# Five waits and positions in a kernel of attention and two expert layers: where output rows, gathered blocks, router transposes, weight turns and one router step stand

## The chip, the cores and the metric

The kernel runs on 1 core of a Trainium2 chip. The metric is device time in microseconds (us), the median of several runs. TensorE, VectorE, ScalarE and GpSimd are the core's compute engines (PE, DVE, ACT and POOL in the profile; PEld is TensorE's weight load); SyncE (SP) only issues transfers here.

## What is computed

The reference, cut to its core (4 batches, 8 heads, 512 local and 32 global positions, head size 64; 2,176 tokens of 512 values in all; 2,048 inner values in the first layer, 8 experts of 1,024 in the second):

```python
a = attention(q_l, k_l, v_l, q_g, k_g, v_g)   # window of 32, plus global keys
x = a.transpose(0, 2, 1, 3).reshape(2176, 512)
h = x @ w_in
x = (np.maximum(h, 0) + alpha * np.minimum(h, 0)) @ w_out
logits = x @ w_gate                            # 8 experts
for idx in np.argsort(-logits.flatten()):      # greedy, 272 tokens an expert
    tok, e = idx // 8, idx % 8
    if assigned[tok] < 0 and counts[e] < 272:
        assigned[tok] = e; counts[e] += 1
for e in range(8):
    out[assigned == e] = np.maximum(x[assigned == e] @ w1[e], 0) @ w2[e]
```

## The kernel before, in words

Every product of the two layers is made in three matmuls: an operand is split into a rounded high half and a low half (the helper `split`, lines 72 and 73: a cast on ScalarE, then a subtract on GpSimd or VectorE), and high times high, low times high and high times low are added up in PSUM. The 2,176 tokens are worked in 8 chunks of 272.

The stages, in the order of time. First attention, then mixed with the first half (`hf` 0) of the first layer. When attention is done (about 223 us) the remaining chunks of half 0 go on, and beside them the weights of half 1 are decoded from 64-bit numbers (`decoding`, lines 77 to 93: a load, one ScalarE and four VectorE instructions into a tile `mag`, which has two buffers) and split. They come in 16 parts: 8 of `w_in`, then 8 of `w_out`. The loop at lines 659 to 676 takes one part after every fifth yield of the GEMM generator (a yield comes after six matmuls). A `w_out` part also returns two closures: `turn_` (line 132: four transposes of the decoded part into `wt`, TensorE, and a ScalarE copy) and `mul_` (line 139: its product with the gate weights, `wp`). They go into the list `more` and are run from its front when it is longer than a limit; what is left runs after the loop. The order of TensorE in this stage, and that of all other engines in every later stage, is made by a scheduler at build time from planned durations, with program order as priority.

Next the first GEMM of half 1 for all 8 chunks (`gemm1b`), with logits of the router (`logits` line 284; `lput`, lines 287 to 297: ScalarE copies to `Lrow`, transposes on TensorE into `l`, a VectorE reduction). Then its second GEMM (`gemm2b`, L1195), in two passes of two output tiles, each over eight operand tiles `f`. From here on the order of TensorE is that of the program. The list `post` holds closures (the last chunk's `lput`, then each chunk's row transposes) that are run behind certain operand tiles.

Mixed into it is the router: eight phases, each picking one expert and its tokens by a threshold search of six steps (`pc`, L907, and `pa`, L919), then `pq` and, but for the last, `pr` (L986), which carries the count of tokens taken; the list of an expert's tokens (`pl` L852, `ps` L859) follows within the next phase. It is a generator that yields planned times in us: `WB` and `WA` around the search steps, `WQ` before `pq`, `WR0` (first phase) or `WR` before `pr`, `WL` in the listing. The GEMM generators yield 0.113 a matmul, and `advance` takes that off the router's planned time; at zero its next instructions are emitted.

Last come eight expert slots. Slot `k` has 8 tiles `up` (L1068, 12 matmuls each) and 4 tiles `down` (L1084, 24 each). Behind the first up tiles it emits the output rows of slot `k - 1` (`emit`): two blocks of four transposes (`ox`, L1115; one PSUM buffer for both), a ScalarE copy into `orow` (L1116) and a scatter on GpSimd's queue (L1118). At the beginning of a slot the token rows of the next are fetched (`fetch_x`, L1018, GpSimd's queue, one buffer `xg`); they are turned in three blocks by `gather` (`xt`, L1054), which begins when the slot's planned time `n` is over `GA` and at least 5 after the fetch, with 2.2 between blocks. Each block is split to `xsh` (ScalarE) and `xsl` (VectorE). The weights of later slots are loaded and split meanwhile (`fetch_1`, `fetch_2`: casts on ScalarE, subtracts on GpSimd). Before slot 0 TensorE runs matmuls of no use (`idle`, L108) while the first rows arrive.

Of the kernel before, what the change touches and what calls it, by code (L numbers as in the profile page):

```python
# [25 lines left out]
def tile_attention_moe_moe(ctx: ExitStack, tc: tile.TileContext, qkw, vw,  # L26
# [133 lines left out]
    def loadx(c, hf):  # L160
        cs = slice(c * CH, (c + 1) * CH)
        X[c, hf] = [None, None]
        if hf:
            t = gx.tile([128, 2, KD, CH], F32, name="xb", bufs=2)
            for i, src in enumerate((xs, xpart)):
                nc.sync.dma_start(out=t[:, i], in_=src[:, :, cs].rearrange("k p t -> p k t"))
                X[c, hf][i] = t[:, i]
# [10 lines left out]
    post = []  # L178
# [21 lines left out]
    def gemm(c, hf, nxt):  # L200
        if len(X[c, hf]) < 3:
            splitx(c, hf)
        if nxt is not None:
            loadx(*nxt)
        gh = gt_.tile([128, KH, CH], F32R, name="ghi", tag="ghi")
        gl = gt_.tile([128, KH, CH], F32R, name="glo", tag="glo")
        wo = WO[hf]
        for f in range(KH):
            g = gh_.tile([128, CH], F32, name="g")
            yield from gemm1(c, hf, f, g)  # L210
            split(gh[:, f], gl[:, f], g, lo_eng=P)
            if post:
                post.pop(0)()
            yield 0.7
        if (c + 1, hf) in X:
            splitx(c + 1, hf)
        ys = {}
        for d, fs in [(0, range(KH - 2)), (1, range(KH - 2)), (0, range(KH - 2, KH)), (1, range(KH - 2, KH))] + [
                (d, range(KH)) for d in range(2, KD)]:
            if d not in ys:  # L220
                ys[d] = ybank[0].tile([128, CH], F32, name="y", tag=ybank[1])
            ps = ys[d]
            ds_ = slice(d * 128, (d + 1) * 128)
            for f in fs:
                for i, (w, x) in enumerate(((0, gh), (0, gl), (1, gh))):
                    T.matmul(ps, wo[:, w, f, ds_], x[:, f], start=f == 0 and i == 0, stop=f == KH - 1 and i == 2)  # L226
                if f % 2 == 1 and f < KH - 1:
                    yield 0.7
            if fs[-1] < KH - 1:
                continue  # L230
            xd = gx.tile([128, CH], F32, name="xd", bufs=2)
            A.copy(xd, ps)
            nc.sync.dma_start(out=xpart[d, :, c * CH:(c + 1) * CH], in_=xd)
            yield 0.7
        X[c, hf] = None
# [78 lines left out]
    with ExitStack() as at:  # L314
# [308 lines left out]
        c = 0  # L623
        g = None
        going = True
        while going:
# [12 lines left out]
            else:  # L639
# [4 lines left out]
                else:  # L644
                    spent["g"] += x
                    if parts:
                        f, i = parts.pop(0)
# [7 lines left out]
    with tc.tile_pool(name="dc2", bufs=1, side="right") as dc, tc.tile_pool(name="pW", bufs=2, space=PSUM) as pW, \  # L655
            tc.tile_pool(name="pO", bufs=2, space=PSUM) as pO:
        odd.append((pO, "h3"))
        more = []
        parts = [(win_part, i) for i in range(2 * KD)] + [(wout_part, i) for i in range(KH)]
        n = 0  # L660
        while c < NCH:
            if g is None:
                if (c, 0) not in X:
                    loadx(c, 0)
                g = gemm(c, 0, (c + 1, 0) if c + 1 < NCH else None)
            while next(g, None) is not None:
                n += 1
                if n % 5 == 0 and parts:
                    f, i = parts.pop(0)
                    with tc.issue_after(epi[0].ins):  # L670
                        todo = f(dc, 1, i)
                    while len(more) > 2:
                        more.pop(0)()
                    more += todo or []
            g = None
            c += 1
        for f, i in parts:
            more += f(dc, 1, i) or []
        for f in more:
            f()  # L680
    NDEF = 8
    DEF = list(range(NCH - NDEF, NCH))
    with ExitStack() as mo:
# [144 lines left out]

        listed, closed = [0], [0]
        WB, WA = (1.7, 2.7, 1.8, 1.8, 1.8, 1.8), (1.7, 1.3, 1.3, 1.3, 1.3, 1.3)  # L830
        WQ, WR0, WR, WL = 2.7, 6.0, 4.2, 1.2

        def listing(k, pos):
            ra = rt.tile([128, NT], F32, name="ra")
# [261 lines left out]
        def turned(k, m):  # L1096
            d = SLOT[k]
            for q, (a, b) in enumerate(SEG):
                if m == 0:
                    pool, tag = ((px, "tx"), (pm, "sm"), (pm, "sm"))[q]  # L1100
                    d["t", q] = pool.tile([128, DM], F32, name="ox", tag=tag)
                T.transpose(d["t", q][:, m * 128:(m + 1) * 128], tail["o"][:, m] if q == 2 else d["o"][:, m, a:b], ident)
# [22 lines left out]
        def slot(k):  # L1125
            d = SLOT[k]
            d["h"] = (sl.tile([128, K3, CAP], F32R, name="hh"), sl.tile([128, K3, CAP], F32R, name="hl"))
            em = emit(k - 1) if k else iter(())
            for f in range(K3):
                yield from up(k, f)  # L1130
                yield 0.113
                if f < 4:
                    yield next(em, 0)
            d["up"] = True
            d["o"] = sl.tile([128, KD, CAP], F32, name="ot")
            if k == 0:
                tail["o"] = sl.tile([128, KD, 128], F32, name="otail", bufs=1)
            for m in range(KD):
                for i, x in enumerate(down(k, m)):
                    if k == E - 1 and m and i == 15:  # L1140
                        turned(k, m - 1)
                    yield x
                yield 0.113
            if k == E - 1:
                turned(k, KD - 1)
# [17 lines left out]
        HB = {}  # L1163
        NB0 = 12
        SLK, SLK2 = 1.0, 1.0
        GA = 17.5
        mo.enter_context(tc.manual_schedule(engines={mybir.EngineType.PE}))

        def splitg(c, f):
            h, l = (gr[:, t, (KH * DEF.index(c) + f) % NR] for t in range(2))  # L1170
            split(h, l, gbt(c, f), lo_eng=P)
            HB.setdefault(c, []).append((h, l))
# [6 lines left out]
        def gemm2b(c):  # L1179
            xo = X[c, 1]  # L1180
            nxt = [lambda f=f: splitg(c + 1, f) for f in range(KH)] if c + 1 < NCH else []
            if nxt:
                loadp(c + 1)
            wo = WO[1]
            end = c == NCH - 1
            if "x" not in tail:
                tail["x"] = gb_.tile([128, KD, 16 * (NCH - 1)], F32, name="xtail")
            for d2 in range(0, KD, 2):
                ps = [(p4 if d2 else pH).tile([128, CH], F32, name="h2", tag="h4" if d2 else "h1") for _ in range(2)]

                def step(f, j):
                    hi, lo = HB[c][f]
                    ds_ = slice((d2 + j) * 128, (d2 + j + 1) * 128)
                    for a, (w, x) in enumerate(((0, hi), (0, lo), (1, hi))):
                        T.matmul(ps[j], wo[:, w, f, ds_], x, start=f == 0 and a == 0, stop=f == KH - 1 and a == 2)  # L1195
                        if a < 2 or not j:
                            yield 0.113

                def add(j):
                    V.tensor_tensor(xo[:, d2 + j], ps[j], xo[:, d2 + j], op=OP.add)  # L1200

                if end and d2:
                    for j in range(2):
                        for f in range(KH):
                            for x in step(f, j):
                                yield None if j else x
                            if j and f == 4:
                                last_blocks(xo, range(KD - 1))
                        add(j)
                    last_blocks(xo, [KD - 1])  # L1210
                    last_out()
                    return
                for f in range(KH):
                    for j in range(2):
                        yield from step(f, j)
                    if (f % 2 == 1 if c != DEF[0] else d2 or f) and post:
                        post.pop(0)()
                        yield 0.4
                    if nxt and ((d2 == 0 and f % 2) or (d2 and f >= 2)):
                        nxt.pop(0)()  # L1220
                    yield 0.113
                for j in range(2):
                    add(j)
            for q in range(3):
                post.append(lambda q=q: rows(c, xo, q))
            if c == NCH - 2:
                post.append(tails)
# [53 lines left out]
        for k in range(E):  # L1281
# [3 lines left out]
            for x in slot(k):  # L1285
# [3 lines left out]
                nx = SLOT.get(k + 1, {})  # L1289
                if gath is None and "at" in nx and n > GA and n > nx["at"] + 5.0:  # L1290
                    gath = gather(k + 1)
# [94 lines left out]
```

## Time and profile before

| | us |
|---|---|
| median of 3 runs | 852.39 (851.32 to 853.04) |
| the profiled execution | 849.98 |
| its span, first to last instruction | 848.2 |
| TensorE busy in it | 807.7 |
| VectorE, ScalarE, GpSimd busy | 473.8, 388.7, 348.7 |

The profile is of one execution. A row of the waits says who waited, for whom, how long in all, how many times, and the longest; only waits over 0.15 us are counted. A row of the timeline has the start, the duration, the engine, the line, the operation with its tiles and shapes, how many were merged, and in brackets the idle time before it and what ended it. A matmul's end is modelled, and successive matmuls overlap.

### The profile page before, as it was taken

What the parts mean: (1) busy time and instruction counts of PE and PEld (TensorE: products, weight loads), DVE (VectorE), ACT (ScalarE), POOL (GpSimd) and SP (SyncE); (2) the same over time, 40 slices, a digit from 0 to 9 for tenths busy, and PEclk for the clock granted to TensorE, in tenths of its full rate; (3) what the DMA queues carried; (4) which work ended last, traced back from release to release, by engine and by line L of the source; (5) the groups of instructions that cost most, each with busy time, mean ns of one, the idle gap of its engine ahead of it and who ended that gap; (6) DMA issues with size and microseconds to landing.
All of it is one profiled execution on the core that took longest, in us unless ns stands there. A gap on an engine that the chain in (4) does not pass through costs nothing. (4 is left out here: it accounts for less than half of the span.)

```text
span 848.2 us, 21036 instructions
## 1 busy us (share of the span) xinstructions
PE 807.7 (95%) x8380; PEld 742.6 (88%) x8380; DVE 473.8 (56%) x1672; ACT 388.7 (46%) x970; POOL 348.7 (41%) x299
## 2 busy tenths in 40 slices
PE   6989999999998999999999999999899999899995
PEld 4767788988998999998989899998689999899995
DVE  5899955464299741252433466776577677711120
ACT  5786655574455643322322434341355544454431
POOL 1134322020255632120000638470599868778601
PEclk9999999999999999999999999999999999999998
DMA  9975552531355302013221227242376655656201
GB/s 343 384 283 199 192 163 70 216 128 48 109 151 168 111 28 80 27 54 90 69 58 50 81 66 263 65 139 81 90 220 205 185 180 163 195 152 210 91 26 38
DMA packets 47993, 115.99 MB, mean 137 GB/s; under 512 B 4183, under 2 KB 20951, under 8 KB 45847
## 3 DMA queue, kind: packets, MB, share of 16 engines
q1 hardware_dynamic: 44999, 105.73, 38.5%
q0 software_dynamic: 2896, 8.92, 3.2%
q8 instruction: 66, 1.08, 0.5%
q14 instruction: 32, 0.26, 0.1%
HBM read 96.80 MB, written 17.83 MB: 135 GB/s over the span
## 5 line engine op out<-in xcount | busy, mean ns | idle before, releaser
L192 PE MATMUL h<-xh,win 128*128 128x272 f32 x768 | 162.4, 298 | 3.1 <-ACT win L72 1.2
L73 POOL TENSOR_TENSOR m<-raw,m 128x1024 fp32r<-128x1024 f32 x64 | 151.8, 2397 | 18.0 <-ACT m L72 10.0
L192 PEld LDWEIGHTS h<-xh,win 128*128 128x128 f32 x768 | 125.1, 190 | 12.7 <-issue 5.1
L192 PE MATMUL h<-xl,win 128*128 128x272 f32 x384 | 111.7, 292 | 1.4 <-DVE xl L73 1.4
L73 POOL TENSOR_TENSOR glo<-g,ghi 128x272 fp32r<-128x272 f32 x64 | 54.5, 857 | 139.3 <-ACT ghi L72 137.8
L226 PE MATMUL y<-ghi,wout 128*128 128x272 f32 x512 | 109.5, 298 | 1.4 <-ACT wout L72 1.4
L1195 PE MATMUL h<-gr,wout 128*128 128x272 f32 x768 | 108.6, 294 | 0.0
L1068 PE MATMUL h<-xsh,m 128*128 128x272 f32 x512 | 106.0, 295 | 0.4 <-ACT xsh L72 0.4
L1084 PE MATMUL h<-hh,m 128*128 128x272 f32 x512 | 102.8, 293 | 0.0
L73 POOL TENSOR_TENSOR gr<-gb,gr 128x272 fp32r<-128x272 f32 x64 | 48.1, 775 | 132.1 <-ACT gr L72 131.5
L1195 PEld LDWEIGHTS h<-gr,wout 128*128 128x128 f32 x768 | 99.4, 189 | 0.6 <-ACT gr L72 0.4
L226 PEld LDWEIGHTS y<-ghi,wout 128*128 128x128 f32 x512 | 83.0, 188 | 6.8 <-issue 3.6
L197 ACT ACTIVATE neg<-h 128x272 f32<-128x272 f32 x128 | 49.8, 395 | 80.9 <-PE h L192 79.0
L1068 PEld LDWEIGHTS h<-xsh,m 128*128 128x128 f32 x512 | 82.4, 188 | 1.5 <-issue 0.8
L1084 PEld LDWEIGHTS h<-hh,m 128*128 128x128 f32 x512 | 81.7, 188 | 1.3 <-issue 1.3
L72 ACT CAST m<-raw 128x1024 fp32r<-128x1024 f32 x64 | 65.4, 1048 | 29.2 <-DMA raw<-in_moe_w_dram 29.1
L1084 PE MATMUL h<-hl,m 128*128 128x272 f32 x256 | 75.4, 295 | 0.0
L1068 PE MATMUL h<-xsl,m 128*128 128x272 f32 x256 | 74.4, 291 | 1.0 <-issue 0.6
L192 PEld LDWEIGHTS h<-xl,win 128*128 128x128 f32 x384 | 72.9, 190 | 2.2 <-DVE xl L73 2.2
L226 PE MATMUL y<-glo,wout 128*128 128x272 f32 x256 | 73.8, 291 | 0.9 <-POOL glo L73 0.9
L198 DVE SCALAR_TENSOR_TENSOR gb<-neg,al,h 128x272 f32<-128x272 f32 x64 | 31.5, 496 | 76.3 <-ACT neg L197 64.4
L400 ACT ACTIVATE pr<-sc,mx 128x128 f32<-128x128 f32 x128 | 49.9, 392 | 32.3 <-DVE mx L398 32.3
(233 smaller groups left out, 1522.0 us busy)
## 6 DMA issues: line engine op xcount, KB each, us to landing
raw<-in_moe_w_dram SPq DMA_DIRECT2D x64, 512.0 KB, 3.7
vv<-in_v_dram SPq DMA_DIRECT2D x16, 1024.0 KB, 8.4
qk<-in_qk_dram SPq DMA_DIRECT2D x14, 720.0 KB, 8.3
raw<-in_moe_w_in_dram SPq DMA_DIRECT2D x16, 512.0 KB, 5.6
raw<-in_moe_w_out_dram SPq DMA_DIRECT2D x16, 512.0 KB, 3.8
xs<-xb SPq DMA_DIRECT2D x16, 272.0 KB, 6.3
xpart<-xd SPq DMA_DIRECT2D x32, 136.0 KB, 3.1
xb<-xs SPq DMA_DIRECT2D x8, 544.0 KB, 3.9
```

The source lines that it names most:

```text
L72: a = A.copy(hi, src)
L73: return a, (lo_eng or V).tensor_tensor(lo, src, hi.bitcast(F32), op=OP.subtract)
L192: T.matmul(ps, wi[:, w, k, fs], x[:, k], start=i == 0, stop=i == 3 * KD - 1)
L197: A.activation(out=neg, in_=ps, func=AF.Relu, scale=-1.0)
L198: epi[0] = V.scalar_tensor_tensor(g, neg, al1[:, hf * KH + f:hf * KH + f + 1], ps, op0=OP.mult, op1=OP.add)
L226: T.matmul(ps, wo[:, w, f, ds_], x[:, f], start=f == 0 and i == 0, stop=f == KH - 1 and i == 2)
L400: A.activation(out=d["pr", j][:, ii], in_=sc, func=AF.Exp, bias=d["mx", j][:, ii:ii + 1], scale=-1.0, accum_out=d["sm", j][:, ii:ii + 1])
L1068: T.matmul(ps, d["w1"][:, w, kk, fs], x[:, kk], start=i == 0, stop=i == 3 * KD - 1)
L1084: T.matmul(ps, d["w2"][:, w, f, ms], x[:, f], start=i == 0, stop=i == 3 * K3 - 1)
L1195: T.matmul(ps[j], wo[:, w, f, ds_], x, start=f == 0 and a == 0, stop=f == KH - 1 and a == 2)
```

## The change

Five numbers or conditions change, each at its own place:

```diff
@@ decoding the weights of half 1 @@
-                    while len(more) > 2:
+                    while len(more) > 4:
                         more.pop(0)()
                     more += todo or []
@@ the router's planned times @@
-        WQ, WR0, WR, WL = 2.7, 6.0, 4.2, 1.2
+        WQ, WR0, WR, WL = 2.7, 6.0, 5.7, 1.2
@@ slot @@
                 yield from up(k, f)
                 yield 0.113
-                if f < 4:
+                if f % 2 == 0:
                     yield next(em, 0)
@@
-        GA = 17.5
+        GA = 15.5
@@ gemm2b @@
-                    if (f % 2 == 1 if c != DEF[0] else d2 or f) and post:
+                    if (f % 2 == 1 if c != DEF[0] else d2 or f > 3) and post:
                         post.pop(0)()
                         yield 0.4
```

The limit of the list of turns and products goes from 2 to 4 entries. The planned time before `pr` is 1.5 longer in the phases after the first. The second block of a slot's output rows is emitted behind up tile 3 of the next slot (counted from 1) where it was behind tile 2. The gathering of the next slot's rows may begin at 15.5 where it was 17.5. In the first chunk of the second GEMM the waiting closure (the last chunk's `lput`) runs behind the fifth operand tile where it ran behind the second.

## Rows read from the trace of the kernel before

**Rows 1.** The page's first part: busy us (share of the span) xinstructions.
```profile
PE 807.7 (95%) x8380; PEld 742.6 (88%) x8380; DVE 473.8 (56%) x1672; ACT 388.7 (46%) x970; POOL 348.7 (41%) x299
```

**Rows 2.** Waits of TensorE, 604 to 840 us: total, times, longest.
```profile
PE ox L1115 <- ACT orow L1116: 1.8, 3, 0.8
PE pl L852 <- DVE sbs L847: 1.4, 1, 1.4
PE pr L986 <- DVE r L981: 1.2, 2, 0.7
PE pa L919 <- DVE sat L912: 0.8, 1, 0.8
PE pc L907 <- DVE gs L873: 0.7, 1, 0.7
PE h L1068 <- issue: 0.6, 1, 0.6
```

**Rows 3.** Waits of TensorE, 362 to 604 us.
```profile
PE l L296 <- ACT Lrow L291: 1.7, 1, 1.7
```

**Rows 4.** Waits of TensorE, 220 to 362 us.
```profile
PE h L192 <- DVE xl L73: 1.4, 2, 1.0
PE wt L135 <- DVE mag L92: 1.4, 1, 1.4
```

**Rows 5.** The chain of waits, slots 2 and 5: start, us, what.
```profile
680.63 0.38 PE pc L907 x9
...
771.52 6.43 PE h L1084 x51
```

**Rows 6.** Timeline of TensorE around the start of slot 1.
```profile
633.59 0.29 PE L1084 MATMUL h<-hl,m 128*128 128x272 f32 x1
...
634.81 0.42 PE L1054 MATMUL xt<-ident,xg 16*128 16x16 f32 x4
635.66 0.39 PE L1068 MATMUL h<-xsh,m 128*128 128x272 f32 x1 [0.43 <-ACT xsh L72]
636.44 0.39 PE L1068 MATMUL h<-xsl,m 128*128 128x272 f32 x1 [0.38 <-DVE xsl L73]
```

**Rows 7.** Timeline of ScalarE, 471 to 477 us.
```profile
471.27 4.57 ACT L72 CAST gr<-gb 128x272 fp32r<-128x272 f32 x14
475.74 0.43 ACT L291 COPY Lrow<-lp 128x144 f32<-128x144 f32 x2
```

**Rows 8.** Timeline of GpSimd, 471 to 483 us.
```profile
471.77 10.20 POOL L73 TENSOR_TENSOR gr<-gb,gr 128x272 fp32r<-128x272 f32 x14 [105.39 <-ACT gr L72]
```

**Rows 9.** Line 859, the router's listings: min/median/max ns, first to last start.
```profile
L859 PE MATMUL ps<-lb,spread x8: 182/183/197, 534.6 to 742.7; 128*128 128x48 bf16 x8
```

**Rows 10.** Slot 6: PE, PEld, DVE, ACT, POOL busy, PEclk, DMA.
```profile
784.90:812.45 27.55, 26.73 (x214) 26.34 (x213) 5.05 (x11) 10.75 (x22) 13.95 (x9) 1.00 0.21 66
```

**Rows 11.** Timeline of ScalarE at the start of slot 5.
```profile
759.92 1.05 ACT L72 CAST m<-raw 128x1024 fp32r<-128x1024 f32 x1
...
761.15 0.58 ACT L1116 COPY orow<-ox 128x512 f32<-128x512 f32 x1
```

**Rows 12.** Timeline of TensorE: the first turn and a late product.
```profile
270.39 0.66 PE L135 MATMUL wt<-ident,mag 128*128 128x128 f32 x4 [1.40 <-DVE mag L92]
...
354.64 0.95 PE L142 MATMUL wp<-ag,wts 128*128 128x8 f32 x8
```

**Rows 13.** Timeline of VectorE, 264 to 272 us: decoding.
```profile
265.62 0.69 DVE L90 SCALAR_TENSOR_TENSOR mag<-raw,mag 128x512 int32<-128x512 int32 x1
...
266.96 0.42 DVE L85 TENSOR_SCALAR mag<-mag 128x512 f32<-128x512 f32 x1
...
267.88 1.73 DVE L90 SCALAR_TENSOR_TENSOR mag<-raw,mag 128x512 int32<-128x512 int32 x1
```

**Rows 14.** Timeline of GpSimd: a weight subtract and the next stage's constants.
```profile
267.78 1.28 POOL L73 TENSOR_TENSOR win<-mag,win 128x512 fp32r<-128x512 f32 x1 [2.47 <-ACT win L72]
...
360.56 0.13 POOL L703 IOTA ip<- 128x1 int32 x1 [16.87 <-PE wp L142]
```

## The prediction

> **What bounds the kernel now.** I read the page's busy times first: TensorE is busy 807.7 us of a span of 848.2, and no other engine comes near [rows 1]. So the end is set by TensorE's own stream of matmuls, and the question is only which gaps in that stream go or come. Next I read the waits of TensorE in three stretches. Between 604 and 840 us, the eight expert slots, they are few and small: 1.8 us before the second block of output transposes (ox) waiting for ScalarE's copy of the first; 1.2 before pr; 2.9 before the router's other matmuls (pl 1.4, pa 0.8, pc 0.7); 0.6 filed under "issue" [rows 2]. Between 362 and 604 us there is 1.7 us before the router's last put of logits is transposed (l) [rows 3]. Between 220 and 362 us there is 1.4 us before the first weight turn (wt) and 1.4 before operand halves (xl) [rows 4].
>
> What is a gap worth? In a run of 51 matmuls that took 6.43 us one starts every 0.126 us [rows 5], while a single one is shown 0.29 us long [rows 6]. A matmul after a gap starts only after the one before it has ended as well, so a gap that vanishes returns about 0.29 - 0.126 = 0.16 us on top of its idle time.
>
> **The change, part by part.** TensorE's order is written out by hand from the second GEMM of the later half on, with 0.113 planned us for a matmul. I followed the generators with the old and the new numbers; counts of matmuls below come from that.
>
> *Router's transposes.* The last chunk's put (copies to Lrow, then the l transposes) now stands behind 30 matmuls of the second GEMM, not 12. The wait ends when ScalarE has done 14 casts (from 471.27, 4.57 us) and then the Lrow copies, to 476.17 [rows 7]. The 18 matmuls that move ahead of it take 18 x 0.126 = 2.3 us, more than the 1.7 us waited [rows 3, 5]. They need GpSimd's subtracts of the third to fifth tile: 14 took 10.2 us, 0.73 each [rows 8], against 6 x 0.126 = 0.76 of matmuls a tile, so they come just in time and may cost some tenths. Gain 1.75 + 0.16, less 0.2: **1.7 us**; at worst 0, if ScalarE's copies are ordered later by as much. The router starts 18 matmuls later in the stream.
>
> *Longer wait for pr.* From the second phase on pr stands 1.5/0.113 = 13 matmuls later, 1.7 us by 0.126. The two waits seen are 1.2 together, the longer 0.7 [rows 2], so both fit. Gain 1.2 + 2 x 0.16 = **1.5 us**. What queues behind pr on TensorE is the next phase's pc, at the same distance from it, and VectorE's update of the remaining places. The router as a whole ends later by 6 x 1.7 plus the 2.3 above, 12.5 us. Its eight listings run from 534.6 to 742.7 us, and the last is wanted by the slot that starts at 812.45, 70 us after it [rows 9, 10]; the planner never has to force a step. Lateness itself costs nothing. But about one pc (0.38 us for nine) and one pl [rows 5] leave the stretch where TensorE only passes time on idle matmuls and enter slot 0: **-0.5 us**.
>
> *Output rows.* The second ox block moves from behind tile 1 to behind tile 3, 12 matmuls or 1.5 us. In slot 5 a cast of 1.05 us stood on ScalarE ahead of the copy of 0.58, which ended at 761.73 [rows 11]; the longest of the three waits is 0.8 [rows 2], so 1.5 covers it with 0.7 to spare. The scatter behind it moves too, on GpSimd's queue; it stands there behind weight subtracts in every slot and nothing reads its rows. Gain 1.8 + 3 x 0.16 = **2.3 us**, at worst 0 if ScalarE puts another cast ahead.
>
> *Gathered blocks.* They start 2.0 planned us, 18 matmuls, earlier. Their last block then stands 23 matmuls before a slot's end, not 5, and 14 before the end of slot 0, where it stood at the very end. There the first up matmul waited 0.43 us for the high half and the next 0.38 for the low half: 1.2 us from the transposes' end at 635.23 to the low half's use at 636.44 [rows 6]. 14 matmuls give 1.77 us, 23 give 2.9. The 0.6 under "issue" [rows 2] is the same wait in slot 3, by its place two matmuls into the slot. Gain 0.43 + 0.38 + 0.59 + 3 x 0.16 = **1.9 us**; 0.2 off, since slot 0 has only 0.6 us to spare and router work on VectorE can stand in front. GpSimd's next row fetches wait for these transposes (the gathered tile has one buffer) and so also come 2.3 us sooner; the weights they share the queue with are a slot ahead, so that is worth nothing.
>
> *Weight turns.* The list holds two entries a part, so a limit of 4 instead of 2 turns each part one step later (five yields, 30 matmuls, 3.8 us), not two. The first turn, at 270.39, waited 1.40 us for VectorE's decode [rows 12]; one step later the decode is done. Gain 1.4 + 0.16 = **1.6 us**. But the decoded tile (mag) has two buffers, and a part's decode waits for the turn two parts before it: it too starts a step later, on VectorE, and SP's queue holds the raw loads behind the decodes. Three parts, not two, are left when the steps end, and the last one's decode waits for a turn that stands behind all remaining chunks: the whole chain then runs at about 355 us or later, where a leftover product stands now: 3.4 us of decode (from 266.96 to the turn's start), a turn of 0.66, a product of 0.95 [rows 12, 13]. The constants of the next stage already wait for these products (GpSimd 16.87 us) [rows 14]. I cost this at 0.3, since the up matmuls of the next stage cover it and VectorE is slack there; without that cover it is the chain itself, 3.4 + 0.66 + 0.95 = 5 us.
>
> What remains uncosted is how the router's other waits (2.9 us now) fall once every phase lies elsewhere in its slot. The nearest rows are those waits; from -2.9 (all gone) to +12. I take +0.4: the router now stays until the end of slot 4, one slot longer.
>
> **Sum.** -1.7 - 1.5 + 0.5 - 2.3 - 1.7 - 1.6 + 0.3 + 0.4 = -7.6 us. The profiled execution took 849.98 us (span 848.2), so it would become 842.4; it lies 2.4 below the median of the runs shown, 852.39, against which I state the time: **844.8 us**. A measurement of this kernel tells about 0.2%, 1.7 us, from no change.
>
> **A rule against the trace.** VectorE's third decode instruction took 1.73 us in one part and 0.69 in another [rows 13]; beside the first GpSimd's subtract of the previous part ran from 267.78 to 269.06 [rows 14]. Moving decodes by a step changes which of them meet a subtract: between no collision and one more, 1.0 us a part, for five parts. The Trainium skill (SBUF — State Buffer, section "Who interferes with whom") says that a VectorE instruction with two SBUF inputs and a GpSimd instruction that reads SBUF exclude each other for the whole instruction. By that rule the later decodes would be stretched whenever they meet GpSimd's subtracts of the first GEMM; the row agrees that such a stretch exists. What it would do to the time is the first rival.
>
> **Rivals.**
> 1. *The weight turns give nothing back or cost.* Decodes a step later run into GpSimd's subtracts, 5 x 1.0 us on an engine that is already late there (the xl waits, 1.4 us [rows 4]), or TensorE stands for the last part's chain of 5 us. For it: the list of three left over. Against it: the next stage has slack on all engines but TensorE. The gain of 1.6 goes and some 3 come: 844.8 + 4.6 = 849.4.
> 2. *ScalarE closes the gaps again.* Its order is made by a scheduler from planned durations. If weight casts of 1.05 us [rows 11] again stand ahead of the copies of ox and of the gathered halves, 2.3 + 1.7 go: 848.8.
> 3. *Slower: the router's waits multiply.* In slots 0 to 4 each phase has twelve pc and pa, a pl and a ps, each tied to a fixed count of matmuls after VectorE's work. At the new places they meet the slot's own VectorE work. If each of five phases had one wait of each size now seen (1.4 + 0.8 + 0.7 = 2.9 [rows 2]), they would be 14.5 instead of 2.9, 11.6 more: 856.4. It decides from 9.3 us more (7.6 + 1.7). Against it: the present phases show about one such wait each at most.
> 4. *Nothing to be seen.* The gaps removed are taken up by later waits, for the transfer or VectorE work that would have ended the next wait anyway: 852.
>
> **Chances.** The forecast 0.58, its own range 842 to 848; rival 1 0.12, rival 2 0.10, rival 4 0.10, rival 3 0.10. The first three are faster by over 0.2%: 0.80; within it 0.10; slower 0.10. The range reaches from 841.0 (the router's other waits mostly gone too) to 851.0, past rivals 1 and 2; rivals 3 and 4 are what it leaves out.
>
> **What would show it.** No wait at l near 476 us, and none at ox in slots 4 to 6; the last xt block some 23 matmuls before each slot's end and no wait at the first up matmul; pr with no wait; the first wt without the 1.4 us. Slots 5 and 6, 27.55 us for the latter [rows 10], should come to about 26.6. Wrong would be: a sum of router waits in slots 0 to 4 well over 4 us, a wait before logits near 360 us, or the same gaps under other names.

## The result and the profile after

The median went from 852.71 us (4 runs, 851.32 to 855.06) to 843.80 (4 runs, 840.38 to 844.62): a ratio of 0.9916, with an interval of 0.9887 to 0.9944. A later measurement of the same two kernels gave 849.94 (12 runs) and 843.63 (7 runs), ratio 0.9928, interval 0.9902 to 0.9955. Neither interval reaches 1, so the changed kernel is faster; the medians differ by 8.9 and 6.3 us, on either side of the 7.6 that were forecast, and 843.80 lies inside the range of 841.0 to 851.0. The question for the experiments is whether the terms of the sum were right one by one.

The profiled execution took 843.68 us (span 841.7), 6.3 less than the one of before. The page's busy times of after:

```profile
PE 808.9 (96%) x8380; PEld 745.1 (89%) x8380; DVE 473.6 (56%) x1672; ACT 389.0 (46%) x970; POOL 347.9 (41%) x299
```

Against [rows 1] the work is the same and TensorE's busy time is even 1.2 us longer, so whatever was won was idle time of TensorE. A table of stages shows where: attention; the rest of half 0 with the first GEMM of half 1; its second GEMM; the idle matmuls; the eight slots. The columns are start and end, length, busy us (and instructions) of TensorE, its weight loads, VectorE, ScalarE and GpSimd, then TensorE's granted clock, the DMA engines' busy share and GB/s. First the kernel before:

```profile
3.34:208.93 205.59, 194.36 (x3116) 160.34 (x3116) 145.69 (x601) 128.09 (x431) 43.58 (x44) 0.99 0.58 207
208.93:472.54 263.61, 259.66 (x2218) 244.26 (x2195) 124.02 (x243) 105.82 (x246) 64.26 (x72) 1.00 0.26 80
472.54:591.08 118.54, 115.57 (x1064) 112.32 (x1064) 78.47 (x327) 42.02 (x93) 66.00 (x71) 1.00 0.40 121
591.08:605.17 14.09, 11.64 (x78) 6.26 (x75) 7.99 (x29) 2.81 (x6) 3.33 (x4) 0.88 0.27 81
605.17:839.43 234.26, 226.23 (x1934) 219.36 (x1933) 116.98 (x472) 107.63 (x194) 166.02 (x91) 1.00 0.50 152
```

And the changed one:

```profile
3.30:212.97 209.67, 198.75 (x3115) 164.05 (x3116) 145.79 (x601) 128.69 (x431) 43.30 (x45) 0.97 0.57 203
212.97:476.60 263.63, 259.68 (x2218) 244.29 (x2195) 124.70 (x243) 105.78 (x245) 63.59 (x72) 1.00 0.26 80
476.60:591.69 115.09, 114.56 (x1053) 111.77 (x1053) 74.38 (x314) 41.99 (x93) 65.96 (x71) 1.00 0.41 124
591.69:604.24 12.55, 9.95 (x72) 5.21 (x69) 6.65 (x23) 3.23 (x6) 3.74 (x4) 1.00 0.30 89
604.24:832.96 228.72, 225.74 (x1955) 219.76 (x1951) 121.42 (x492) 106.92 (x194) 165.85 (x91) 1.00 0.51 156
```

Line by line: attention is 4.1 us longer, though nothing of it was changed; its mean clock is 0.97, not 0.99. The first GEMM stage, in which the weight turns stand, is the same to 0.02 us. The second GEMM is 3.4 shorter, the idle stretch 1.5, the slots 5.5. From the start of the second GEMM to the last output transposes that is 366.9 before and 356.4 after, 10.5 us less, of which attention's clock took 4.1 back in this execution.

The waits of TensorE between 604 and 840 us, to be read against [rows 2] (total, times, longest):

```profile
PE pl L852 <- DVE sbs L847: 1.3, 2, 1.0
PE ox L1102 <- ACT ot L1091: 0.5, 1, 0.5
PE pq L966 <- DVE m L956: 0.3, 1, 0.3
PE h L1068 <- ACT xsh L72: 0.3, 1, 0.3
PE pr L986 <- DVE r L981: 0.2, 1, 0.2
PE pc L907 <- DVE gs L873: 0.2, 1, 0.2
```

The second ox block (L1115) waits no more, and the up matmuls (h, L1068) wait 0.3 where 0.6 stood under "issue"; pr has 0.2 left of 1.2. The ox of L1102 is the block at the very end of the kernel. The router's four waits and pq are 2.0 together, where they were 4.1.

Slot 6, by the same columns as [rows 10]:

```profile
780.46:806.98 26.52, 26.52 (x214) 26.34 (x213) 5.05 (x11) 10.62 (x23) 11.96 (x7) 1.00 0.17 60
```

It was 27.55 with 26.73 busy; now it is busy from end to end. The prediction had 26.6.

Between 212 and 604 us the longest waits are, to be read against [rows 3, 4]:

```profile
PE xt L1054 <- issue: 2.6, 1, 2.6
PE h L192 <- DVE xl L73: 1.4, 2, 1.0
PE wt L135 <- DVE mag L92: 1.4, 1, 1.4
...
```

The wait at l is gone; the 2.6 at xt, the first gathered block, was 2.45 before. The wait at the first weight turn, which the change was to remove by the prediction, stands there with the same 1.4 us. The timeline of TensorE and of ScalarE around those two places (start, duration, operation; in brackets the idle time before):

```profile
274.41 0.66 PE L135 MATMUL wt<-ident,mag 128*128 128x128 f32 x4 [1.40 <-DVE mag L92]
...
480.45 0.49 PE L296 MATMUL l<-ident,Lrow 128*128 128x128 f32 x3
```

```profile
475.34 4.57 ACT L72 CAST gr<-gb 128x272 fp32r<-128x272 f32 x14
479.81 0.43 ACT L291 COPY Lrow<-lp 128x144 f32<-128x144 f32 x2
```

ScalarE still does 14 casts and then the Lrow copies, as in [rows 7], and ends at 480.24; l comes at 480.45 with no gap. For the turn, 274.41 less the 4.04 us by which the stage starts later is 270.37: the same place as the 270.39 of [rows 12].

### The profile page after: what moved, and what is told of

Same layout as the page of the kernel before. It is cut to its first block, busy times and chain, and to the rows that moved or that the text cites. A ratio compares the mean times of both kernels' runs of the same rounds, so it can differ in the third digit from the quotient of the medians.

```text
span 841.7 us, 21041 instructions
## 1 busy us (share of the span) xinstructions
PE 808.9 (96%) x8380; PEld 745.1 (89%) x8380; DVE 473.6 (56%) x1672; ACT 389.0 (46%) x970; POOL 347.9 (41%) x299
## 4 chain that ended last, share of the span: by engine, by line
PE 53%; issue 7%; POOL 4%; DVE 3%; DMA 2%; ACT 1%; POOLq 0%; DVEq 0%
PE h L192 16%; PE h L1195 12%; PE h L1084 7%; PE h L1068 6%; PE y L226 5%; POOL m L73 3%; PE lp L284 2%; DMA raw<-in_moe_w_dram 2%; PE pc L907 1%; PE xt L1054 1%; PE idle L108 1%; PE wp L142 1%; PE yt L247 1%; POOL xg L1018 1%; POOL out_dram L1118 1%
## 5 line engine op out<-in xcount | busy, mean ns | idle before, releaser
L192 PE MATMUL h<-xh,win 128*128 128x272 f32 x768 | 164.7, 300 | 2.9 <-ACT win L72 1.1
L73 POOL TENSOR_TENSOR m<-raw,m 128x1024 fp32r<-128x1024 f32 x64 | 152.1, 2401 | 12.8 <-ACT m L72 10.5
L1068 PE MATMUL h<-xsh,m 128*128 128x272 f32 x512 | 105.0, 295 | 0.3 <-ACT xsh L72 0.3
L1068 PEld LDWEIGHTS h<-xsh,m 128*128 128x128 f32 x512 | 82.1, 188 | 0.5 <-ACT xsh L72 0.5
L1068 PE MATMUL h<-xsl,m 128*128 128x272 f32 x256 | 74.6, 291 | 0.0
```

The source lines that it names most:

```text
L73: return a, (lo_eng or V).tensor_tensor(lo, src, hi.bitcast(F32), op=OP.subtract)
L192: T.matmul(ps, wi[:, w, k, fs], x[:, k], start=i == 0, stop=i == 3 * KD - 1)
L1068: T.matmul(ps, d["w1"][:, w, kk, fs], x[:, kk], start=i == 0, stop=i == 3 * KD - 1)
```

## The experiments

Each part alone was run once. The times move by several us with attention's clock, so these runs are read by the stage that a part touches, against the two tables above. In what follows the router's waits are those at pc, pa, pq, pr, pl and ps in the slots.

**Weight turns alone** (the kernel before with one edit):

```diff
-                    while len(more) > 2:
+                    while len(more) > 4:
```

> Only the limit of the list of weight turns goes from 2 to 4. Theory: the scheduler puts the first turn where TensorE would otherwise stand in its own plan, whatever the program order, so the wait of 1.4 us at the first turn stays, and the stretch from the last score matmul of attention to the first matmul of the second GEMM stays at 263.6 us (it was 263.61 before and 263.63 after). Rival, the prediction's step: the wait goes and the stretch is about 262 us.

The time was 853.25 us, beside 850.02 of the kernel before. The stage that holds the turns (window of that stage, then the wait in it):

```profile
211.69:475.43 263.74, 259.76 (x2218) 244.29 (x2194) 124.74 (x243) 105.81 (x245) 63.62 (x72) 1.00 0.25 80
```

```profile
PE wt L135 <- DVE mag L92: 1.4, 1, 1.4
```

263.74 is 0.13 more than before, and the first turn waits its 1.4. The edit gives nothing, and costs nothing that can be seen there. The slots took 235.0, 0.7 more, with router waits of 4.9 for 4.1. That is no effect of the edit: from before slot 0 on, all four engines run the same instructions in the same order in both traces. It is the scatter from one execution to the next. Three profiles of the changed kernel's order (the one above, and two further ones below) lie between 228.7 and 229.1, with router waits of 1.6 to 2.4.

**Router's transposes alone:**

```diff
-                    if (f % 2 == 1 if c != DEF[0] else d2 or f) and post:
+                    if (f % 2 == 1 if c != DEF[0] else d2 or f > 3) and post:
```

> Only the router's first transposes stand behind five operand tiles. The stretch from the first matmul of the second GEMM to the first up matmul was 132.6 us before and 127.6 after. Theory: the wait at l (1.7 us) goes, worth 1.9, and the whole router stands 18 matmuls later, so that the wait of 0.6 us at a chunk's second row block goes too, 0.8; without a low clock in the idle stretch (1.5) the stretch is then 128.4, with one 129.9. Rival: only l's own 1.9 is gained, 130.7 with the low clock, and the row wait stays.

849.53 us beside 850.02. The window of the second GEMM:

```profile
476.49:591.78 115.29, 114.76 (x1054) 111.86 (x1054) 77.06 (x325) 41.94 (x93) 65.78 (x71) 1.00 0.39 124
```

It is 3.2 shorter than before, of the 3.4 of the full change, with 10 matmuls fewer in the window (1064 before). So the part works, and this stage's gain is this edit's, within the 0.5 by which the stage scatters (below). The slots took 234.5: with the router later, its waits fell to 2.5, but the second ox block now waited 4.0 in all, where it had 1.8.

**Longer wait for pr alone:**

```diff
-        WQ, WR0, WR, WL = 2.7, 6.0, 4.2, 1.2
+        WQ, WR0, WR, WL = 2.7, 6.0, 5.7, 1.2
```

> Only the longer wait before pr. The stretch from the first up matmul to the last output transposes was 234.3 us before and 228.7 after. Theory: the pr waits (1.2 us) go and the other router waits (2.9 us) fall to about half, so 231.5 to 233. Rival: the other waits come back at other places and the stretch stays at 234.

854.74 us beside 850.02. Window and first waits of the slots:

```profile
607.24:844.09 236.85, 227.88 (x1950) 221.22 (x1948) 119.69 (x483) 106.91 (x194) 166.06 (x91) 0.99 0.48 151
```

```profile
PE ox L1115 <- ACT orow L1116: 3.4, 5, 0.8
PE pl L852 <- DVE sbs L847: 1.8, 1, 1.8
PE pc L907 <- DVE gs L873: 1.6, 2, 1.1
PE h L1068 <- ACT xsh L72: 1.1, 1, 1.1
```

The waits at pr are gone, but pl and pc have more than [rows 2] had, ox 3.4 for 1.8, and xsh 1.1 more. The stretch is 2.6 us longer, not 1.5 shorter, and neither the expectation's theory nor its rival. But 3.4 us of it ran at half the clock:

```profile
746.10:749.50 3.40, 3.40 (x17) 3.28 (x16) 1.79 (x10) 2.83 (x4) 1.42 (x1) 0.50 0.40 142
```

The same 18 matmuls of slot 4 took 3.92 us here (with one ps among them) and 2.27 in the kernel before, so the clock cost some 1.6. Without it the edit alone costs some 1.0, little over the scatter of 0.7; it gives nothing here.

**Gathered blocks alone:**

```diff
-        GA = 17.5
+        GA = 15.5
```

> Only the gathered blocks begin at 15.5 instead of 17.5. Theory: the three waits at the first up matmuls of slots 1 and 3 (1.4 us) go, worth 1.9 us: the stretch from the first up matmul to the last output transposes goes from 234.3 to about 232.4 us. Rival: the waits move to the blocks' own transposes or to the output rows, and the stretch stays within 0.5 us of 234.3.

846.61 us beside 850.02. The slots:

```profile
605.50:836.05 230.55, 225.43 (x1934) 219.01 (x1933) 117.19 (x472) 108.10 (x194) 166.34 (x91) 1.00 0.49 155
```

```profile
PE ox L1115 <- ACT orow L1116: 2.2, 4, 0.8
PE pc L907 <- DVE gs L873: 1.1, 2, 0.7
PE pl L852 <- DVE sbs L847: 0.5, 1, 0.5
```

3.7 us less, where 1.7 was forecast. No up matmul waits at a slot's start any more, and the router's waits came to 2.2, from 4.1. Neither this profile nor that of before had the clock fall in the slots.

**Output rows alone:**

```diff
-                if f < 4:
+                if f % 2 == 0:
```

> Only the second block of output rows moves behind tile 3. Theory: the waits at ox (1.8 us before, up to 4.0 in the runs of other single edits) go, and the stretch from the first up matmul to the last output transposes falls from 234.3 to about 232 us; slots 5 and 6 fall from 27.5 to 26.5 each. Rival: ScalarE still has a cast in front, some ox wait stays, and the stretch is above 233.5.

851.02 us beside 852.06 (7 runs). The slots:

```profile
607.07:840.47 233.40, 226.81 (x1935) 221.06 (x1933) 116.89 (x472) 107.54 (x194) 166.01 (x91) 0.99 0.50 153
```

```profile
PE pa L919 <- DVE sat L912: 2.0, 3, 0.8
PE h L1068 <- ACT xsh L72: 1.1, 1, 1.1
```

Its own wait, 1.8, is wholly gone, but the stretch is only 0.86 shorter: pa, 0.8 before, has 2.0, the xsh of a slot's start 1.1, and 3.4 us ran at half the clock:

```profile
639.90:643.30 3.40, 3.40 (x25) 3.33 (x24) 0.75 (x3) 2.33 (x4) 2.93 (x3) 0.50 0.67 216
```

The same instructions, from the 9th to the 23rd up matmul of slot 1, took 4.37 us here and 2.90 in the kernel before. The clock thus cost 1.47, and without it the part gave some 2.3. Slots 5 and 6, in which no router stands, show it undisturbed: 26.5 each, where all six kernels with the second block behind tile 2 took 27.5.

**All but the longer wait for pr** (the changed kernel with the old number):

```diff
-        WQ, WR0, WR, WL = 2.7, 6.0, 5.7, 1.2
+        WQ, WR0, WR, WL = 2.7, 6.0, 4.2, 1.2
```

> The changed kernel with the old planned time before pr (4.2). Alone the longer wait gave nothing: the stretch from the first up matmul to the last output transposes was 236.9 us with it, 234.3 without. Theory: beside the other edits it is worth nothing or costs; the stretch is 227.5 to 229.5 (228.7 in the changed kernel), the time within 1.5 us of 843.8. Rival: the pr waits come back (1.2 us) with one or two other router waits and the stretch is 230.2 or more, the time about 845.5.

843.10 us (4 runs, 842.64 to 846.9), ratio to before 0.9896 (0.9846 to 0.9946): not to be told from the changed kernel. The slots took 1.5 us more than with the edit, which is the expectation's rival, though its time isn't:

```profile
601.74:831.93 230.19, 225.17 (x1945) 219.35 (x1941) 117.62 (x479) 107.54 (x194) 165.71 (x91) 1.00 0.50 155
```

```profile
PE pc L907 <- DVE gs L873: 1.7, 4, 0.7
PE pl L852 <- DVE sbs L847: 1.5, 2, 0.7
PE pr L986 <- DVE r L981: 0.7, 1, 0.7
```

pr has 0.7 of 4.5 of router waits; the others grew more than pr did. That fits a theory in which the places of all the router's steps count, and pr's number only as one way of moving them. Two further runs test that, below.

**Turns queued behind the last matmul written.** In the program the first turn follows 966 matmuls of half 0's GEMMs before and 996 after, 30 later, as the prediction counted. In both traces it stands after 949 of them, 517 of the first GEMM and 432 of the second, where the program has 486 (516 after) and 480. So TensorE's order, which the scheduler makes here, isn't the program's. This kernel is the changed one with the turn tied to the last matmul written ahead of it (`mm[0]` is set at each matmul of both GEMMs):

```diff
-                for k in range(KD):
-                    T.transpose(t[:, k], val[:, k * 128:(k + 1) * 128], ident)
+                with tc.issue_after(mm[0].ins):
+                    for k in range(KD):
+                        T.transpose(t[:, k], val[:, k * 128:(k + 1) * 128], ident)
```

> The changed kernel, and each part's turn queued on TensorE behind the last matmul traced before it, so that it stands where the list puts it. Theory: the first turn's wait of 1.4 us goes, worth 1.6, and the stretch from the last score matmul of attention to the first matmul of the second GEMM falls from 263.6 to about 262 us. Rival: VectorE is the bound there, the 1.4 us comes back at another matmul of the stretch (xl, g or glo), and it stays at 263.6. A turn that stands behind all remaining chunks holds the last part's decode: if TensorE has to wait for it, the stretch is longer by up to 5 us.

842.51 us (4 runs, 841.59 to 843.98), ratio 0.988 (0.9835 to 0.9926), again not to be told from the changed kernel. The stage:

```profile
210.49:474.12 263.63, 259.71 (x2219) 244.31 (x2196) 124.16 (x243) 105.93 (x246) 63.59 (x72) 1.00 0.25 80
```

The first turn is after matmul 949 still, with its wait of 1.4. The matmul that it was tied to is the 516th of the first GEMM in the program, and 517 of them stand ahead of it in the trace: that matmul had itself been taken ahead. So the run didn't move the first turn, and what a later place would give it wasn't seen.

**The router later, nothing else changed** (the kernel before; 2.03 planned us are the 18 matmuls by which moving l delays the router):

```diff
-            yield 3.0
+            yield 5.03
```

> The kernel before, with the router alone started 2.03 planned us (18 matmuls) later and l left at its place. It parts the two things that the move of l did. Theory: the stretch from the first matmul of the second GEMM to the last output transposes of the first layer, 118.3 us in four runs of kernels with l in its old place and 115.3 or 115.1 with the new, falls only by the row block's wait and the router matmuls that leave it: about 117.4, with the wait at l still 1.8. Rival: the stretch stays at 118.2, and all of the 3.1 us came from l itself.

848.09 us beside 850.27. The second GEMM, and the wait in it that moving l removes:

```profile
472.74:590.00 117.26, 114.97 (x1055) 111.84 (x1054) 77.23 (x325) 41.97 (x93) 65.96 (x71) 1.00 0.40 122
```

```profile
PE l L296 <- ACT Lrow L291: 1.8, 1, 1.8
```

The stretch is 1.0 shorter than the median of the five kernels with l and the router at the old place (118.24; 118.09 to 118.54), with the l wait still in it. So of the 3.0 to 3.2 that moving l gives, 1.0 comes from the router's shift (fewer of its matmuls in the stretch, and a wait of 0.2 to 0.6 at a row transpose gone), and the rest, some 2.0, is the wait itself, beside the 1.75 + 0.16 of the prediction's working. That is one profile, against a scatter of 0.5 among the five.

**The changed kernel with the router 13 matmuls later still:**

```diff
-            yield 3.0
+            yield 4.5
```

> The changed kernel with the router started 1.5 planned us (13 matmuls) later, so that each of its steps lies elsewhere in its slot. Theory: the router's waits in the slots depend on where its steps fall, not on pr's wait alone: they come to anything from 1.5 to 5 us (2.1 in the changed kernel, 4.1 before), and the stretch of the slots to 228.5 to 232 us. Rival: the longer wait for pr has settled them, and they stay within 0.7 us of 2.1, the stretch within 0.8 of 228.7.

844.28 us beside 850.27. The slots:

```profile
603.27:833.56 230.29, 225.99 (x1960) 219.95 (x1958) 121.11 (x493) 107.65 (x194) 166.13 (x91) 1.00 0.51 155
```

```profile
PE pr L986 <- DVE r L981: 1.8, 1, 1.8
```

A single wait of 1.8 stands at pr, in spite of the longer planned time: 1.5 more does not cover it wherever it falls. The slots left the rival's range and stayed in the theory's.

**The same shift with the old wait for pr:**

```diff
-            yield 3.0
+            yield 4.5
...
-        WQ, WR0, WR, WL = 2.7, 6.0, 5.7, 1.2
+        WQ, WR0, WR, WL = 2.7, 6.0, 4.2, 1.2
```

> The same shift of 1.5 planned us, with the old wait before pr. Its router waits were 4.5 us without the shift and the slots 230.2. Theory: the shift deals them anew, 2 to 5 us, and pr's own share of them is 0.4 to 1.2. Rival: the old wait before pr always costs, so that the router waits stay above 4 us and the slots above 229.8.

842.58 us beside 850.27. The slots:

```profile
603.11:831.88 228.77, 225.22 (x1950) 219.86 (x1948) 119.62 (x483) 107.77 (x194) 166.07 (x91) 1.00 0.50 156
```

As short as the changed kernel's 228.72, with no wait at pr at all under the old number, less than even the theory gave it. The longer number goes with slots 1.5 shorter at one place of the router and 1.5 longer at the other, each a single profile but twice the scatter. So no gain of pr's number by itself shows: at one place of the router 4.2 waits 0.7, at another nothing; 5.7 waits 0.2 at one and 1.8 at another.

**Idle matmuls up to the first rows.** Before slot 0 TensorE waits 2.6 us ahead of the first xt, behind its 12 groups of idle matmuls. This kernel is the changed one with 17:

```diff
-        NB0 = 12
+        NB0 = 17
```

> The changed kernel with 17 instead of 12 rounds of idle matmuls before the first gathered rows: ten more of 0.22 us fill 2.2 of the 2.6 us in which TensorE stands before the first transposes (xt). The low clock at the beginning of slot 0 came in seven of the twelve profiles so far and made the stretch from the last transposes of the first layer to the first up matmul 13.8 to 14.2 us, without it 12.2 to 12.6. Theory: the gap is what lets the clock fall there, so it stays high in the profile, the stretch is about 12.5 us, and the median falls by about 1 us against the changed kernel run beside it. Rival: the idle matmuls run past the rows' arrival or the clock falls all the same, and nothing is gained.

840.64 us (6 runs, 839.27 to 845.26), ratio 0.9908 (0.9879 to 0.9936) to the kernel before, run beside it.

```profile
588.64:601.20 12.56, 12.45 (x92) 6.58 (x89) 9.54 (x34) 3.22 (x6) 3.74 (x4) 1.00 0.29 91
```

The gap is filled, 12.45 busy of 12.56, and the stretch is as long as without the fill (12.55). The first xt begins 8.2 us after the stretch's start, as in the other profiles (8.15 to 8.30), so it is the rows' arrival that sets it. The clock stayed up, as it did without the fill in all three profiles of the changed kernel's order. That the fill keeps it up is not shown.

**The changed kernel again**, unchanged, beside it:

> The changed kernel again, beside the one above: 842 to 845 us by the eight timed runs so far of it and of the kernel with the turns queued behind (840.4 to 844.6), and at the same granted clock 7 to 8 us under the kernel before; the stretch of the slots 228.7 to 229.1, router waits 1.6 to 2.1 us.

843.63 us (7 runs, 840.3 to 846.43), ratio 0.9928 (0.9902 to 0.9955). Its stages repeat the first profile's (second GEMM 115.10, idle 12.55, slots 228.71); the router's waits, 2.4, are a little over what was expected. The intervals of this kernel and of the filled one overlap, so 840.64 beats the kernel before, but isn't shown to beat the changed one.

## Why the prediction was right, and which steps were not

The sum was -7.6, and the two measurements gave -8.9 and -6.3; its terms did not all come out. By stage, between the two profiles: the slots were forecast at -4.6 (pr, output rows, gathered blocks, the router's other waits and the matmuls that come in) and took 5.5 less; the second GEMM at -1.7, and took 3.4 less; the stage of the weight turns at -1.3, and took the same. Attention and the idle stretch were forecast at nothing and moved by +4.1 and -1.5 with the clock.

**Router's transposes, -1.7: right, under-sized.** The wait went as described: ScalarE's order held, the 18 matmuls covered it, GpSimd's subtracts kept up. It measured some -2.0 for the wait and another -1.0 for the router's later start, which the prediction had counted only as some matmuls that leave for the slots, not as a shorter stretch here.

**Output rows, -2.3: right.** No wait is left at ox in slots 1 to 7 of the changed kernel (0.3 in the one with the router later still). Slots 5 and 6 lost 1.0 each, and alone the part gave some 2.3 once the half clock is taken off. In the kernels that keep the second block behind tile 2, its waits range from 1.8 to 4.0 us, so the part protects more than the one profile of before showed.

**Gathered blocks, -1.7: right place, too small.** -3.7 alone. The last block stands 14 matmuls before the end of slot 0 and 23 before the others', as counted, and the waits at the slots' starts went but for 0.3 in slot 1 of the changed kernel. What the term lacked is that the router's waits fell by 1.9 as well, over twice their scatter. Why they fell so was not tried.

**Longer wait for pr, -1.5: failed.** The step that failed is "The two waits seen are 1.2 together, the longer 0.7, so both fit. Gain 1.2 + 2 x 0.16". It took waits of one arrangement for properties of the instruction. Over the 14 profiles the router's waits come to 1.6 to 5.1 us in all, under pc, pa, pl, pq and pr by turns, and they change with every edit that moves any of the stream. Even one order of instructions gave 4.1 and 4.9 of them, another 1.6, 2.0 and 2.4. Alone the slots took 2.6 more, 1.6 of it the clock's; taken back out of the change, 1.5 more; with the router shifted the sign turns (230.3 with it, 228.8 without).

**Router's other waits, +0.4: wrong sign.** All router waits together went from 4.1 to 2.0. They belong in one term with pr: -2.1, against the -1.1 forecast for the two, though the gathered blocks alone gave 1.9 of it. Rival 3, the multiplying of these waits to 14.5, did not come; the largest seen is 5.1.

**Matmuls moved into the slots, +0.5: right in kind.** By their starts, 16 more of the router's matmuls lie in the slots: nine pc and five pl, the ones that were counted, and two pa. (The table's 1955 for 1934 has some that run across its edge.) What they cost there was not measured by itself.

**Weight turns, -1.6 and +0.3: both failed.** The step is "one step later the decode is done". It followed the program's order, in a stage where a scheduler makes TensorE's. The first turn did not move by one matmul, and what it waits for is VectorE's decode, which nothing in the change makes earlier. Most of that wait is one stretched instruction, in the changed kernel as in [rows 13]:

```profile
271.90 1.73 DVE L90 SCALAR_TENSOR_TENSOR mag<-raw,mag 128x512 int32<-128x512 int32 x1
```

At the 0.69 of another part it would have ended 1.04 sooner, of the 1.40 waited. The Trainium skill (SBUF — State Buffer, section "Who interferes with whom") says that a VectorE instruction with two SBUF inputs contends with a GpSimd instruction that reads SBUF. The trace agrees: GpSimd's subtract ran beside this one from 271.80 to 273.09.

The other seven turns did move, by 3.0 to 44 us against the stage's start, and the late chain that the prediction described came. The last instruction of the decodes (count, min/median/max ns, first to last start), before and after:

```profile
L92 DVE SCALAR_TENSOR_TENSOR mag<-raw,mag x16: 677/692/840, 234.8 to 303.8; 128x512 int32<-128x512 int32 x16
L92 DVE SCALAR_TENSOR_TENSOR mag<-raw,mag x16: 678/692/695, 238.8 to 351.9; 128x512 int32<-128x512 int32 x16
```

The last part's decode is 44 us later, beyond the 4.0 by which the stage starts later. Its price was nothing, neither the 0.3 nor the 5 us without cover: the stage is 263.6 to 263.8 in every profile. Of rival 1 the lost gain came true and its reason did not: the decodes were stretched no more than before (their four VectorE instructions took 51.8 us in all before and 50.8 after), and TensorE didn't stand for the chain.

**Not in the sum:** the idle stretch, -1.5, and attention's +4.1 in this execution, both of the clock (last section). That the total came out near is in part luck, errors that cancel: -3.1 forecast for pr and the first turn, of which neither edit gave its part, against some -3.3 too little for l and the gathered blocks.

## What to carry to other kernels

In a hand-written order that has several chains woven in, a wait belongs to the arrangement, not to the instruction: cost such an edit by the stage's total. Before reading a part's gain from a stage, take off what the clock did in it and ask how far the same order scatters. In the slots the parts alone gave +0.3 (router's transposes), +2.6 (pr), -3.7 (gathered blocks) and -0.9 (output rows), which is -1.7 beside -5.5 for all together, as if they worked only in company. With the two half-clock stretches off, +2.6 is some +1.0 and -0.9 is some -2.3, and the sum is -4.7. With single profiles that scatter by 0.7 each, these runs don't show that the parts fail to add up.

The sure gains here were slack before a fixed point: a slot's start, the reuse of a buffer, a transpose that waits for a copy. And before costing a move in program order, find the instruction's place in the trace: where a scheduler makes the order, the very instruction that is to move may stay, while others move.

## What the runs showed of the hardware

In 7 of the 14 profiles the clock of TensorE fell to half (0.50 granted, 1.2 GHz of 2.4) for 3.4 us near the first xt, ahead of slot 0, in the kernel before thus:

```profile
600.40:603.80 3.40, 3.40 (x22) 1.96 (x20) 1.70 (x4) 0.81 (x2) 0.00 (x0) 0.50 0.03 7
```

Ahead of it the engine had done idle matmuls, stood 2.45 us for the rows, and done one block of xt and some idle matmuls. The changed kernel stood 2.60 us there and kept its clock. The stretch is 13.8 to 14.2 us with the fall and 12.2 to 12.6 without, some 1.5 us. What decides it is open. In the order of the kernel before it came in all four profiles, and in that of the changed kernel in none of three. But in a third order, the same in the runs with the router's transposes alone, with the late router and without the longer wait for pr, it came in the last of them only, with the instructions and a standstill of 2.3 to 2.4 us alike. So the same order goes either way, and whether the change has a part in the 1.5 is not shown.

In attention the changed kernel's profile had two such stretches, the other one of 3.4 us from 93.4. TensorE was busy throughout the longer:

```profile
55.90:66.10 10.20, 10.12 (x88) 8.17 (x88) 6.79 (x17) 7.17 (x24) 3.13 (x4) 0.50 0.83 308
```

They come before any instruction that the change touches. Attention took 205.2 to 209.7 us over the 14 profiles, and the spread between runs of one kernel goes with the clock: in the last measurement the kernel before took 846.29 to 850.30 at a mean clock of 0.994 to 0.995 and 849.57 to 852.08 at 0.989 to 0.991. What sets these falls was not tried and stays open.
